# An mLSTM cell followed by a SwiGLU block: when k and q are first turned by 32 by 32 tiles, where weight words are joined, and the order of the first group

## The chip, the cores and the metric

The kernel runs on one core of a Trainium2 chip. The metric is the device time of one execution in microseconds (us); the time shown for a kernel is the median of its runs. A profiled execution is a further one, recorded by the hardware profiler; its span goes from the first to the last instruction. The engines are called as in the profile: PE multiplies matrices (PEld loads its stationary operand), DVE, ACT and POOL compute elementwise, and SP only issues transfers here. ACT also issues some transfers on its own queue.

## What is computed

```python
# q, k, v, o_gate: (4, 8, 768, 40) float32; i_gate, f_gate: (4, 8, 768) float32
for t in range(S):
    m_new = np.maximum(f_gate[:, :, t] + m, i_gate[:, :, t])
    f_stab, i_stab = np.exp(f_gate[:, :, t] + m - m_new), np.exp(i_gate[:, :, t] - m_new)
    m = m_new
    C = f_stab[:, :, None, None] * C + i_stab[:, :, None, None] * np.einsum('bhd,bhe->bhde', vt, kt)
    n = f_stab[:, :, None] * n + i_stab[:, :, None] * kt
    h_tilde = np.einsum('bhde,bhe->bhd', C, qt)
    denom = np.maximum(np.abs(np.einsum('bhd,bhd->bh', n, qt)[:, :, None]), 1.0)
    y[:, :, t] = h_tilde / (1.0 + np.exp(-o_gate[:, :, t])) / denom
x = y.transpose(0, 2, 1, 3).reshape(3072, 320)
g = x @ w_gate                      # (320, 1536), float64 in memory
out = (g / (1.0 + np.exp(-g)) * (x @ w_val)) @ w_out      # (3072, 320)
```

## The kernel before

The 768 time steps are cut into six groups of 128. For each group the cell is computed in its chunked form and gives 4 times 128 rows of x; `seam` turns them into xT; `hidden(g, m)` computes one twelfth of the hidden layer of a group (20 matrix instructions into two PSUM banks, then `AF.Silu` on ACT into `sg`, then a product on DVE); `project` or, in group 0, `project_all` multiplies with w_out, and `result` copies each of four blocks to `z_sb` on ACT and sends it out on SP. PE thus runs hidden(g, 0) to hidden(g, 11), then the projection of group g, and the cell of group g+1 is put between the hidden blocks of group g, in the lists `slots` and `after`, which say behind which block a step is written. Nothing reorders what is written: each engine's queue is run in the order of the program text, and `ahead` says which weight block is converted ahead of which hidden block.

PSUM has two rings of four banks. "gen" serves `hidden`, `project` and the first group's values; "cell" serves the scores, the state, the turns and the seams.

The weights come as 64-bit words and are made into float32 by integer steps. `piece_load(p)` brings a piece (the gate half on SP, the value half on ACT, both lines L161). `scale(j)` makes `top` and `low` from the two words of block j on ACT (L186, L188). `join(j)` makes `both` from `top` on DVE (L196, L197). `rounded(j)` adds `low` into the weight tile, on POOL or, for some blocks, on DVE (L204). The tiles `top`, `low` and `both` have one buffer each. Pieces 0 and 1 hold weight blocks 0 and 1, pieces 2 to 6 two blocks each, pieces 7 to 9 are w_out (blocks 12 to 17).

k and q are needed with the feature axis on the partitions. Group 0 does this with `first_turn` on PE, group 1 with `turn` (32 matrix instructions of PE and four copies for half of the heads), and groups 2 to 5 with `turn_squares`: the transfers of `load_squares` (16 for q and 16 for k, each a strip of 32 by 32 or 32 by 8 numbers) bring the data so that DVE's 32 by 32 transpose alone is enough. q's squares lie in `q_sb`, k's in `k_sq`.

The first group has its own functions (`first_mask` to `first_seam`), written between L540 and L582. `burn(n)` gives PE n idle products. `late_sums` and `late_maxima` prepare the gates of the five later groups, `late_turns` and `decay_rows`/`decay` what these need of it. `sig` is the sigmoid of the output gates on ACT.

Every transfer carries one of eight completion counters, in turn; a transfer that takes a counter waits for the transfer that had it before. The wait stands on the queue that issues it, so that on ACT the computing instructions written behind it wait too.

Of the kernel before, what the change touches and what calls it, by code (L numbers as in the profile page):

```python
# [11 lines left out]
I32 = mybir.dt.int32  # L12
# [12 lines left out]
def kernel(  # L25
# [102 lines left out]
    nc.sync.dma_start(out=i0, in_=spread_rows(i_gate))  # L128
    nc.scalar.dma_start(out=flat(f_sb), in_=gate_rows(f_gate)[:, L:])
    nc.scalar.dma_start(out=flat(i_sb), in_=gate_rows(i_gate)[:, L:])  # L130

# [3 lines left out]

    def piece_load(p, home=None):
        kind, m, n = PIECES[p]
        if kind == "gv":
            a, d = NKC, n * 128
            src = [(slice(i * HP, (i + 1) * HP), w[:, m * 128:(m + n) * 128].rearrange("(c p) f -> p c f", p=HP))  # L140
                   for i, w in enumerate((moe_w_gate, moe_w_val))]
            queues = (nc.sync, nc.scalar)
        else:
            a, d = n, DM
            src = [(slice(0, 128), moe_w_out[m * 128:(m + n) * 128].rearrange("(a p) d -> p a d", p=128))]
            queues = (nc.sync,)
# [34 lines left out]
    def scale(j):  # L181
        if j in blocks:
            lo, hi, dst = blocks[j]
            a, d = hi.shape[1], hi.shape[2]
            top = conv.tile([128, NKC * 128], F32, name="top", bufs=1).rearrange("p (a d) -> p a d", a=a)
            nc.scalar.mul(top, hi.bitcast(F32), 2.0 ** -112)  # L186
            low = conv.tile([128, NKC * 128], I32, name="low", bufs=1).rearrange("p (a d) -> p a d", a=a)
            nc.scalar.mul(low, lo, 2.0 ** -29)  # L188
            blocks[j] = (low, top.bitcast(U32), dst)

    def join(j):
        if j in blocks:
            lo, top, dst = blocks[j]
            a = dst.shape[1]
            both = conv.tile([128, NKC * 128], U32, name="both", bufs=1).rearrange("p (a d) -> p a d", a=a)
            nc.vector.tensor_scalar(both, top, scalar1=3, scalar2=None, op0=ALU.logical_shift_left)  # L196
            nc.vector.scalar_tensor_tensor(both, in0=top, scalar=0x80000000, in1=both, op0=ALU.bitwise_and,  # L197
                                           op1=ALU.bitwise_or)
            blocks[j] = (lo, both, dst)

    def rounded(j, eng=None):
        if j in blocks:
            lo, both, dst = blocks.pop(j)
            (eng or nc.gpsimd).tensor_tensor(dst.bitcast(I32), both.bitcast(I32), lo, op=ALU.add)  # L204

# [9 lines left out]
    load(o_sb, o_gate, 0, 0)  # L215
    load(o_sb, o_gate, 0, 1)

# [223 lines left out]

    def burn(n):
        t = bank("burn")
        for _ in range(n):
# [109 lines left out]
    first_turn(1, q_sb, qT, (A, V))  # L554
    piece_load(0)
    piece_load(1)
    first_own(1)
    first_values(1)
    first_x(1)
    first_scores(1)  # L560
    sig(0)
    sig(1)
    piece_load(2, h_sb[:, NH - NKC:])
    piece_load(3, wo_sb)
    burn(3)
    first_own(2)
    first_own(3)
    first_gate(0)
    first_x(2)
    first_x(3)  # L570
    first_gate(1)
    first_seam(0, (A, V, A))
    scale(0)
    piece_load(4)
    burn(5)
    join(0)
    first_seam(1, (A, A, A))
    rounded(0, V)
    first_state(0, A)
# [100 lines left out]
    def load_all(dst, a, n):  # L680
        for P in range(2):
# [9 lines left out]
    slots = {  # L691
        0: [run(first_state, 1, A), run(load_all, k_sb, k, 1), run(load_all, q_sb, q, 1), run(late_maxima)],
        1: [run(decay_rows), run(piece_load, 6, h_sb[:, NH - NKC:])],
        2: [run(late_turns), run(weights_load, 1)],
        3: [run(decay), run(load_all, v_sb, v, 1)],
        6: [run(turn, 0, (A, A), (A, V)), run(piece_load, 7)],
        7: [run(turn, 1, (A, A), (A, V)), run(weights_sub, 1, 0), run(weights_sub, 1, 1), run(weights_mask, 0),
            run(weights_mask, 1)],
        8: [run(weights_exp, 0), run(weights_exp, 1), run(weigh_values, G, 0), run(weigh_values, G, 1),
            run(piece_load, 8)],  # L700
        9: [run(do_scores), run(do_weigh, 0), run(load_all, o_sb, o_gate, 1)],
        10: [run(do_weigh, 1), run(do_add), run(do_state, 2, 0), run(do_state, 2, 1)],
        11: [run(do_attend, 1, 0), run(do_gather, 1, 0, False), run(piece_load, 9)],
    }
    for m in range(NFC):
        hidden(0, m, [run(convert, j, V if j in on_vector else None) for j in ahead[m]])
        for f in slots.get(m, ()):
            f()
    after = {
        0: [run(do_attend, 1, 1), run(convert, 14), run(sig, 0), run(sig, 1), run(do_gate, 0)],  # L710
        1: [run(do_gather, 1, 1), run(weights_load, 2), run(load_all, v_sb, v, 2),
            run(nc.gpsimd.memset, q_sb, 0.0)],
        2: [run(do_divide, 0), run(convert, 15)],
        3: [run(do_divide, 1), run(load_all, k_sb, k, 2), run(load_squares, q_sq, q, 2), run(load_all, o_sb, o_gate, 2)],
        4: [run(convert, 16), run(seam, 1, 0, (A, V, A, V))],
# [17 lines left out]
    nc.gpsimd.memset(k_sq, 0.0)  # L733
    load_squares(k_sq, k, 2)


    for g in range(1, NG):
        n, f = g + 1, g + 2
        slots = {m: [] for m in range(NFC)}
        if n < NG:  # L740
            slots[2 if g == 1 else 0] = [run(turn_squares, q_sq, qT)]
            slots[2 if g == 1 else 1] += [run(turn_squares, k_sq, kT)]
            slots[3] = [run(do_scores), run(do_weigh, 0)]
# [59 lines left out]
```

## Time and profile before

| what | us |
|---|---|
| median of 3 runs | 574.75 (573.42 to 575.8) |
| profiled execution, whole | 574.24 |
| its span, first to last instruction | 572.5 |
| PE busy with matrix instructions | 562.0 |
| DVE / ACT / POOL busy | 221.9 / 142.9 / 105.8 |
| bytes moved by DMA | 40.46 MB |
| granted TensorE clock, mean | 0.991 |

The span and the time of the profiled execution differ by 1.74 us, which lie outside the instructions. A line of the timeline reads: start, duration, engine, line of the kernel, operation, result and operands with their shapes, count, and in brackets the idle time before it and what ended it. "x40" behind a matrix instruction of L619 stands for two hidden blocks. Instructions of PE are pipelined, so a busy PE may still wait inside a merged line.

### The profile page before, as it was taken

What the parts mean: (1) busy time and instruction counts of PE and PEld (TensorE: products, weight loads), DVE (VectorE), ACT (ScalarE), POOL (GpSimd) and SP (SyncE); (2) the same over time, 40 slices, a digit from 0 to 9 for tenths busy, and PEclk for the clock granted to TensorE, in tenths of its full rate; (3) what the DMA queues carried; (4) which work ended last, traced back from release to release, by engine and by line L of the source; (5) the groups of instructions that cost most, each with busy time, mean ns of one, the idle gap of its engine ahead of it and who ended that gap; (6) DMA issues with size and microseconds to landing.
All of it is one profiled execution on the core that took longest, in us unless ns stands there. A gap on an engine that the chain in (4) does not pass through costs nothing.

```text
span 572.5 us, 11789 instructions
## 1 busy us (share of the span) xinstructions
PE 562.0 (98%) x5151; PEld 326.4 (57%) x5151; DVE 221.9 (39%) x378; ACT 142.9 (25%) x221; POOL 105.8 (18%) x103
## 2 busy tenths in 40 slices
PE   9999998999899999999999999999999999999997
PEld 4955454764555576455567445567455567544475
DVE  5776595870434620434630433640332630011100
ACT  3366554435201115110114201014211010111100
POOL 2132345464101132002132001232001110000000
PEclk9999998999899999999999999999999999999999
DMA  8999992495457620354440263360000000000000
GB/s 124 179 285 179 174 264 93 86 119 104 55 67 88 112 45 24 53 53 72 81 75 24 35 70 49 64 115 24 12 2 1 2 2 26 21 2 0 1 22 24
DMA packets 180987, 40.46 MB, mean 71 GB/s; under 512 B 171496, under 2 KB 176104, under 8 KB 180936
## 3 DMA queue, kind: packets, MB, share of 16 engines
q1 hardware_dynamic: 178356, 35.55, 37.8%
q10 hardware_dynamic: 2580, 4.16, 3.4%
q8 instruction: 40, 0.66, 0.5%
q14 instruction: 11, 0.09, 0.1%
HBM read 35.68 MB, written 4.01 MB: 69 GB/s over the span
## 4 chain that ended last, share of the span: by engine, by line
PE 86%; DMA 5%; SPq 4%; ACT 3%; issue 1%; DVE 1%; POOL 0%; ACTq 0%; DVEq 0%; POOLq 0%
PE gv_ps L619 50%; PE o_ps L635 23%; PE o_ps L642 4%; SPq L113 3%; DMA raw<-in_moe_w_val_dram 3%; DMA h_sb<-in_moe_w_gate_dram 2%; PE inter L369 2%; PE intra L374 2%; PE add L350 2%; PE sp L329 1%; PE tp_x L415 1%; DMA out_dram<-z_sb 1%; DVE w_sb L336 0%; ACT L624 0%; ACT L436 0%
## 5 line engine op out<-in xcount | busy, mean ns | idle before, releaser
L619 PE MATMUL gv_ps<-xT,wgv_sb 64*128 64x512 f32 x1440 | 323.3, 599 | 3.9 <-ACT sg L624 2.8
L619 PEld LDWEIGHTS gv_ps<-xT,wgv_sb 64*128 64x128 f32 x1440 | 142.6, 188 | 161.2 <-issue 151.5
L625 DVE TENSOR_TENSOR h_sb<-sg,gv_ps 128x512 f32<-128x512 f32 x72 | 49.4, 687 | 290.3 <-ACT sg L624 269.3
L635 PE MATMUL o_ps<-wo_sb,h_sb 128*128 128x320 f32 x480 | 130.5, 433 | 0.0
L635 PEld LDWEIGHTS o_ps<-wo_sb,h_sb 128*128 128x128 f32 x480 | 90.8, 190 | 38.2 <-issue 0.8
L624 ACT ACTIVATE sg<-gv_ps 128x512 f32<-128x512 f32 x72 | 42.9, 597 | 264.7 <-PE gv_ps L619 264.7
L359 POOL TENSOR_TENSOR C<-C,dec 128x328 f32<-128x328 f32 x20 | 14.5, 735 | 156.4 <-DVE C L361 156.4
L629 ACT COPY z_sb<-o_ps 128x320 f32<-128x320 f32 x24 | 10.2, 426 | 116.2 <-PE o_ps L635 102.7
L432 POOL TENSOR_SCALAR_AFFINE_SELECT w_sb<-w_sb 64x1024 f32<-64x1024 f32 x20 | 28.1, 1406 | 27.0 <-DVE w_sb L427 26.0
L642 PE MATMUL o_ps<-wo_sb,h_sb 128*128 128x320 f32 x96 | 26.9, 437 | 0.0
L395 POOL TENSOR_TENSOR o_sb<-o_sb,y_sb 128x640 f32<-128x640 f32 x10 | 14.2, 1428 | 48.5 <-DVE y_sb L386 48.5
L642 PEld LDWEIGHTS o_ps<-wo_sb,h_sb 128*128 128x128 f32 x96 | 17.9, 190 | 7.2
L386 DVE TENSOR_TENSOR y_sb<-y_sb,intra 64x328 f32<-64x328 f32 x40 | 19.7, 492 | 1.0
L339 POOL TENSOR_TENSOR vw_sb<-v_sb,w_sb 128x656 f32<-128x656 f32 x10 | 12.8, 1302 | 34.2 <-issue 25.8
L204 POOL TENSOR_TENSOR wgv_sb<-both,low 128x640 int32<-128x640 int32 x8 | 13.4, 1671 | 24.7 <-DVE both L197 24.7
L197 DVE SCALAR_TENSOR_TENSOR both<-top,both 128x640 uint32<-128x640 uint32 x18 | 15.7, 870 | 0.6
L369 PEld LDWEIGHTS inter<-C,qT 64*64 64x64 f32 x640 | 10.2, 134 | 7.3 <-issue 6.8
L389 DVE TENSOR_SCALAR den<-den 128x16 f32<-128x16 f32 x10 | 14.0, 1402 | 0.3
L196 DVE TENSOR_SCALAR both<-top 128x640 uint32<-128x640 uint32 x18 | 10.5, 581 | 8.6 <-ACT top L186 6.7
L350 PEld LDWEIGHTS add<-vw_sb,k_sb 64*64 64x64 f32 x640 | 10.4, 135 | 5.7 <-issue 4.9
L361 DVE TENSOR_TENSOR C<-C,add 128x328 f32<-128x328 f32 x20 | 9.9, 493 | 9.3 <-POOL C L359 9.3
L204 POOL TENSOR_TENSOR wo_sb<-both,low 128x640 int32<-128x640 int32 x6 | 10.2, 1700 | 15.7 <-DVE both L197 12.2
(124 smaller groups left out, 367.0 us busy)
## 6 DMA issues: line engine op xcount, KB each, us to landing
w_sb<-M_dram SPq DMA_DIRECT2D x10, 512.0 KB, 6.2
k_sb<-in_k_dram SPq DMA_DIRECT2D x12, 320.0 KB, 6.4
v_sb<-in_v_dram SPq DMA_DIRECT2D x12, 320.0 KB, 4.9
o_sb<-in_o_gate_dram SPq DMA_DIRECT2D x12, 320.0 KB, 6.7
raw<-in_moe_w_out_dram SPq DMA_DIRECT2D x3, 1280.0 KB, 7.2
out_dram<-z_sb SPq DMA_DIRECT2D x24, 160.0 KB, 1.8
q_sb<-in_q_dram SPq DMA_DIRECT2D x32, 64.0 KB, 2.5
k_sq<-in_k_dram SPq DMA_DIRECT2D x32, 64.0 KB, 2.5
```

The lines of the kernel that those rows point to most:

```text
L113: nc.sync.dma_start(out=dst[:, heads(P), 0:D], in_=tokens(a, c, P))
L197: nc.vector.scalar_tensor_tensor(both, in0=top, scalar=0x80000000, in1=both, op0=ALU.bitwise_and, op1=ALU.bitwise_or)
L204: (eng or nc.gpsimd).tensor_tensor(dst.bitcast(I32), both.bitcast(I32), lo, op=ALU.add)
L350: nc.tensor.matmul(ps[i][half(two), a, :], lhsT=k_sb[half(i), h, :], rhs=vw_sb[half(i), h, :], start=True, stop=True)
L369: nc.tensor.matmul(inter[two][half(i), a, :], lhsT=qT[half(two), P * UA + a, half(i)], rhs=state(2 * n + i)[half(two), P * UA + a, :], sta ...
L386: nc.vector.tensor_tensor(t, t, intra[i][half(c)], op=ALU.add)
L432: nc.gpsimd.affine_select(w, w, compare_op=ALU.is_ge, fill=NEG, base=0, pattern=[[0, UH], [1, SUB]], channel_multiplier=-1)
L619: nc.tensor.matmul(ps[i], lhsT=wgv_sb[half(i), m, PAIRS[kc][i], :], rhs=x[half(i), kc, :], start=(kc == 0), stop=(kc == NKC - 1))
L624: nc.scalar.activation(sg, ps[0], AF.Silu)
L625: nc.vector.tensor_tensor(hid(g, m), sg, ps[1], op=ALU.mult)
L635: nc.tensor.matmul(p, lhsT=hid(g, m)[:, ts(u, L)], rhs=wo_sb[:, m, :], start=(m == 0), stop=(m == NFC - 1))
L642: nc.tensor.matmul(ps[u], lhsT=hid(g, m)[:, ts(u, L)], rhs=wo_sb[:, m, :], start=(m == 0), stop=(m == NFC - 1))
```

## The change

Five things are changed.

1. Group 2 is turned by `turn` on PE in the first two slots of group 1; squares are loaded and used from group 3 on. The loads of q's and k's squares for group 2 (32 transfers) become two plain loads of q (those of k were there already, for the state). The clearing of `q_sb` moves from group 0's projection to behind the second turn.
2. `join` writes into the weight tile itself, and `rounded` adds to it in place; `both` is gone and `low` has two buffers. Block 0 is rounded on POOL and no longer on DVE.
3. The second half of the output gates is loaded behind weight piece 0; the gates of the later groups (`f_sb`, `i_sb`) are loaded from ACT behind `sig(0)` and no longer at the start. The value halves of pieces 2 and 3 are issued on SP and no longer on ACT.
4. In the first group `scale(0)` stands ahead of `sig(1)`, `join(0)` and `rounded(0)` among the last values; `burn(8)` on a "gen" bank replaces `burn(5)` on a "cell" bank; one copy of the second seam goes from ACT to DVE.
5. In the slots of group 0 `late_maxima`, `late_turns`, `decay_rows` and `decay` stand one block later, both turns one block earlier, and the second `do_weigh` one block earlier, behind the first.

```diff
-    nc.scalar.dma_start(out=flat(f_sb), in_=gate_rows(f_gate)[:, L:])
-    nc.scalar.dma_start(out=flat(i_sb), in_=gate_rows(i_gate)[:, L:])
...
-    def piece_load(p, home=None):
+    def piece_load(p, home=None, second=nc.scalar):
...
-            queues = (nc.sync, nc.scalar)
+            queues = (nc.sync, second)
...
-            low = conv.tile([128, NKC * 128], I32, name="low", bufs=1).rearrange("p (a d) -> p a d", a=a)
+            low = conv.tile([128, NKC * 128], I32, name="low").rearrange("p (a d) -> p a d", a=a)
...
-            both = conv.tile([128, NKC * 128], U32, name="both", bufs=1).rearrange("p (a d) -> p a d", a=a)
+            both = dst.bitcast(U32)
...
-            lo, both, dst = blocks.pop(j)
-            (eng or nc.gpsimd).tensor_tensor(dst.bitcast(I32), both.bitcast(I32), lo, op=ALU.add)
+            lo, dst = blocks.pop(j)
+            (eng or nc.gpsimd).tensor_tensor(dst, dst, lo, op=ALU.add)
...
-    load(o_sb, o_gate, 0, 1)
...
     piece_load(0)
+    load(o_sb, o_gate, 0, 1)
     piece_load(1)
     first_own(1)
     first_values(1)
     first_x(1)
     first_scores(1)
     sig(0)
+    nc.scalar.dma_start(out=flat(f_sb), in_=gate_rows(f_gate)[:, L:])
+    nc.scalar.dma_start(out=flat(i_sb), in_=gate_rows(i_gate)[:, L:])
+    piece_load(2, h_sb[:, NH - NKC:], nc.sync)
+    piece_load(3, wo_sb, nc.sync)
+    scale(0)
     sig(1)
-    piece_load(2, h_sb[:, NH - NKC:])
-    piece_load(3, wo_sb)
     burn(3)
     first_own(2)
     first_own(3)
     first_gate(0)
     first_x(2)
+    join(0)
     first_x(3)
+    rounded(0)
     first_gate(1)
     first_seam(0, (A, V, A))
-    scale(0)
+    burn(8, "gen")
     piece_load(4)
-    burn(5)
-    join(0)
-    first_seam(1, (A, A, A))
-    rounded(0, V)
+    first_seam(1, (V, A, A))
     first_state(0, A)
     convert(1)
     piece_load(5)
...
-        0: [run(first_state, 1, A), run(load_all, k_sb, k, 1), run(load_all, q_sb, q, 1), run(late_maxima)],
-        1: [run(decay_rows), run(piece_load, 6, h_sb[:, NH - NKC:])],
-        2: [run(late_turns), run(weights_load, 1)],
-        3: [run(decay), run(load_all, v_sb, v, 1)],
-        6: [run(turn, 0, (A, A), (A, V)), run(piece_load, 7)],
-        7: [run(turn, 1, (A, A), (A, V)), run(weights_sub, 1, 0), run(weights_sub, 1, 1), run(weights_mask, 0),
-            run(weights_mask, 1)],
+        0: [run(first_state, 1, A), run(load_all, k_sb, k, 1), run(load_all, q_sb, q, 1)],
+        1: [run(late_maxima), run(piece_load, 6, h_sb[:, NH - NKC:])],
+        2: [run(weights_load, 1), run(load_all, v_sb, v, 1), run(decay_rows)],
+        3: [run(late_turns)],
+        4: [run(decay)],
+        5: [run(turn, 0, (A, A), (A, V))],
+        6: [run(turn, 1, (A, A), (A, V)), run(piece_load, 7)],
+        7: [run(weights_sub, 1, 0), run(weights_sub, 1, 1), run(weights_mask, 0), run(weights_mask, 1)],
...
-        9: [run(do_scores), run(do_weigh, 0), run(load_all, o_sb, o_gate, 1)],
-        10: [run(do_weigh, 1), run(do_add), run(do_state, 2, 0), run(do_state, 2, 1)],
+        9: [run(do_scores), run(do_weigh, 0), run(do_weigh, 1), run(load_all, o_sb, o_gate, 1)],
+        10: [run(do_add), run(do_state, 2, 0), run(do_state, 2, 1)],
...
-        1: [run(do_gather, 1, 1), run(weights_load, 2), run(load_all, v_sb, v, 2),
-            run(nc.gpsimd.memset, q_sb, 0.0)],
+        1: [run(do_gather, 1, 1), run(weights_load, 2), run(load_all, v_sb, v, 2)],
...
-        3: [run(do_divide, 1), run(load_all, k_sb, k, 2), run(load_squares, q_sq, q, 2), run(load_all, o_sb, o_gate, 2)],
+        3: [run(do_divide, 1), run(load_all, k_sb, k, 2), run(load_all, q_sb, q, 2), run(load_all, o_sb, o_gate, 2)],
...
-    load_squares(k_sq, k, 2)
...
-            slots[2 if g == 1 else 0] = [run(turn_squares, q_sq, qT)]
-            slots[2 if g == 1 else 1] += [run(turn_squares, k_sq, kT)]
+            slots[0] = [run(turn, 0, (A, V), (A, V))] if n == 2 else [run(turn_squares, q_sq, qT)]
+            slots[1] = [run(turn, 1, (A, V), (A, V))] if n == 2 else [run(turn_squares, k_sq, kT)]
+            if n == 2:
+                slots[1].append(run(nc.gpsimd.memset, q_sb, 0.0))
```

## The prediction, written before the changed kernel had run

> **What bounds the kernel now.** I read the shares of the chain first, then the chain in order of time, then PE's timeline wherever PE was idle or slow, and last what the engine named there had been doing.
>
> ```profile
> PE 86%; DMA 5%; SPq 4%; ACT 3%; issue 1%; DVE 1%; POOL 0%; ACTq 0%; DVEq 0%; POOLq 0%
> ```
>
> PE is the chain, and the rest lies at the beginning: in order of time there is nothing but PE from 145 us to the last copy. There a pair of hidden blocks takes 8.78 us (4.39 each) and a projection 26.0, group after group. So the change can gain or lose only at the start of PE's hidden work, at the idle places before 157 us, and by PE work added or taken. These are the places:
>
> ```profile
> 33.45 4.56 PE L619 MATMUL gv_ps<-xT,wgv_sb 64*128 64x512 f32 x20
> 49.59 4.74 PE L619 MATMUL gv_ps<-xT,wgv_sb 64*128 64x512 f32 x20 [0.99 <-POOL wgv_sb L204]
> ...
> 84.94 5.71 PE L619 MATMUL gv_ps<-xT,wgv_sb 64*128 64x512 f32 x20
> 90.58 1.34 PE L350 MATMUL add<-vw_sb,k_sb 64*64 64x41 f32 x64
> 93.33 0.28 PE L350 MATMUL add<-vw_sb,k_sb 64*64 64x41 f32 x2 [1.41 <-DVE w_sb L336]
> 93.94 1.14 PE L350 MATMUL add<-vw_sb,k_sb 64*64 64x41 f32 x62 [0.32 <-DVE w_sb L336]
> 95.00 6.26 PE L619 MATMUL gv_ps<-xT,wgv_sb 64*128 64x512 f32 x20
> ...
> 133.52 8.85 PE L619 MATMUL gv_ps<-xT,wgv_sb 64*128 64x512 f32 x40
> 145.17 11.27 PE L619 MATMUL gv_ps<-xT,wgv_sb 64*128 64x512 f32 x40 [2.80 <-ACT sg L624]
> ```
>
> Measured against 4.39 us a block, hidden(0,10) at 84.94 loses 1.25 (to the start of add at 90.58); add takes 4.49 instead of the 2.0 of later groups and loses 2.5; hidden(0,11) at 95.0 loses 1.8; PE idles 2.80 before 145.17, and the pair after it loses 2.5. With the 0.99 before 49.59 that is 11.8 us. The reader is to see that a slow block follows two of the idle spells, 1.7 us in add and 2.80, and none follows the 0.99 or the 1.25.
>
> Why PE idles at 142.4 is on ACT and SP:
>
> ```profile
> 118.66 11.73 SPq L313 DMA_DIRECT2D q_sb<-in_q_dram  x16
> 130.48 1.83 SPq L113 DMA_DIRECT2D o_sb<-in_o_gate_dram  x2
> 132.46 5.22 SPq L630 DMA_DIRECT2D out_dram<-z_sb  x4
> ```
> ```profile
> 132.01 0.96 ACT L629 COPY z_sb<-o_ps 128x320 f32<-128x320 f32 x2 [9.66 <-PE o_ps L642]
> 136.42 0.80 ACT L629 COPY z_sb<-o_ps 128x320 f32<-128x320 f32 x2 [3.45 <-DMA out_dram<-z_sb]
> 144.52 1.08 ACT L624 ACTIVATE sg<-gv_ps 128x512 f32<-128x512 f32 x2
> ```
>
> Sixteen square loads hold SP for 11.7 us, the output gates are issued behind them, and the first output block (3.86 us to landing in the chain, median 1.8 of all) shares the DMA with these. z has two buffers, so the third copy waits; three table loads, exp and sigmoid stand behind it on ACT, and only then the first Silu, 8.1 us after the third copy began.
>
> **What the Trainium skill says.** "TensorE: Matmul & The Clock Gate", Part 1, says PE's clock falls to half after an idle window of about 3.4 us and needs a busy one to recover, the window running freely. The trace agrees in kind: behind both long spells weight loads take 0.35 or 0.61 us a pair instead of 0.19; it shows 1.7 us of idle among small products as enough. The same Part says ACT and DVE run their queues strictly in order; here ACT stood from 49.00 to 50.17 before issuing piece 6, until piece 5 landed at 50.10. "DMA: Bandwidth & Descriptors", Specifications, wants 512 B for line rate; the squares are strips of 128 and 32 B, the k, q, v and o rows 160 B, and 10:20, full of the latter, moved 153 GB/s where 30:40, full of weights, moved 321. "SBUF — State Buffer", Who interferes with whom, says a DVE instruction with two SBUF inputs contends with POOL; L197 took 0.83 us, and 1.63 beside POOL's masks.
>
> **The change part by part.**
>
> *The start.* Before, hidden(0,0) starts at 33.45, when the seam copies end (33.19). Now ACT's queue decides. The built program's list of waits puts in front of `scale(0)` the load of i_sb, which waits for piece 1's gate half, and in front of the second seam's copies the issue of piece 4's value half, which waits for piece 2's value half. I date both by bytes. o0 landed at 21.2 (issue 14.21, 7.0 to landing); without f_sb, i_sb (0.16 MB, about 0.7 us) and the two value halves that shared from 18.9 (about 1.1 us) it lands near 19.4. Behind it up to piece 1 come 1.31 MB of weights and o1's 0.33 MB: at about 185 GB/s, between 153 and 198 (20:30), 8.8 us, so near 28.2. Piece 2's 1.31 MB at 321 GB/s takes 4.1 more, near 32.5. So scale(0) (1.57) runs from 28.3, sig(1) ends near 30.7; join(0) (1.35) puts x(3), gate(1) (2.0) and the POOL copy at 32.8; the second seam's transposes (1.3) and `first_state` (1.06) bring PE to 35.2, its copies being done at 35.0. burn(8), at 0.4 each as in burn(5)'s 2.02, ends at 31.6 and is hidden under this wait. The start slips by 1.75 us. Bounds: 33.2 if everything landed early enough, 37.5 if the landings slip by 2.3.
>
> *To hidden(0,4).* Before, it starts at 54.88 with the decay product (0.55) done. Now 35.2 + 4 x 4.39 + 1.06 (`first_state`) + 0.8 (`late_turns`) = 54.6, and the decay product is still to come: 55.2. The 0.99 stall goes, since late_maxima (2.8 us of DVE, then exp) no longer stands ahead of block 3. It now stands ahead of block 4: Silu ends near 45.8, the maxima near 49.4, exp 50.1, piece 6's issue 50.7 (it waits for piece 5, which I put at 48 to 50), scale, join and POOL 54.4. That is level with PE, so any slip shows. Net loss 0.3.
>
> *Joining in place.* It removes waits of ACT for POOL (0.8 to 0.95 each) in work beside PE, and 4.39 us of PE a block covers it: nothing, except at blocks 10 and 11, where DVE holds Silu of hidden(0,8). There `low` frees ACT, but weights_sub and POOL's masks still stretch DVE, and I leave the 1.25 us loss as it is. Without that cover it would gain up to 1.25.
>
> *do_weigh one block earlier.* The four products (0.64 each) run at 89.3 to 91.9 ahead of join(12), so add finds its banks and takes 2.0; hidden(0,11) runs 93.1 to 97.5 at full clock instead of ending at 101.2. What is late next: join(12) and Silu's product now stand behind the four products, POOL's block 12 ends near 94.9, and the state chain of POOL and DVE (4.6 us, as from 93.64 to 98.27) ends at 99.4. The second half of attend's banks waits for it, about 1.0 us. attend ends at 100.4, before at 103.2: gain 2.8.
>
> *Group 2's turns.* The 32 square loads leave SP; two q loads (about 2 us each by the k loads' 3.73 for two) replace 11.7 us before the outputs. The first output lands in 1.8 us, the third copy starts at 134.3 on the old scale, Silu of hidden(1,0) ends at 143.0. PE has one turn (1.0) more and reaches the second turn at 143.3. Its banks are freed by ACT's copies behind that Silu and DVE's behind its product: k's at 144.4, q's at 145.1. So hidden(1,2) starts at 145.6, 0.4 later than before, with 2.0 us of turns done, and the pair runs warm, the longest wait being 1.1 us: it ends at 154.4 against 156.45. Gain 2.05. DVE's squares at 152.85 lay beside PE, so taking them gains nothing. The q_sb clearing (1.8 us on POOL) comes at 146, long before the states at 167 and the squares' use past 225.
>
> **Sum.** +0.3 - 2.8 - 2.05 = -4.55 us. On the profiled execution: span 568.0, and with the 1.74 outside it 569.7. The median shown stands 0.5 above the profiled execution, so I forecast 570.2.
>
> **Rivals.**
> Given back to the clock (0.22). The start has 1.3 us of idle and small products ahead of hidden(0,0), attend 1.0, the second turn 1.3: each shorter than the 1.7 that was enough before, but the window runs freely. Each slow window costs 1.8 to 2.5. Two of them: 570.2 + 4 = 574.2, no change. For it: both slow blocks of the trace; against: the 0.99 and 1.25 that had none.
> Slower (0.18). ACT's queue at the start: transfers that wait for landings now stand in front of the seam copies, where before none did. If pieces 1 and 2 land some 6 us later than I reckon (value halves starved by SP's ring, or the 160 B rows at 153 GB/s deciding), hidden(0,0) starts near 41.5 on a cold clock: +6.3 + 1.8 - 4.55 = 3.55, so 578.3. It decides once the start passes 42.6, or 40.8 with the cold window.
> More than the sum (0.12). DVE gets through blocks 10 and 11 in time (1.25) and the turn's banks come free early (up to 1.3), the start slips less (1): 566.7.
> The forecast itself has 0.48, with its own range 568 to 572.5.
>
> **How the numbers follow.** A measurement of this kernel cannot tell less than about 0.5%, 2.9 us, from no change: the borders are 571.9 and 577.6. Faster gets nearly all of the forecast and all of the last rival, 0.58; no change the clock's rival and the edges, 0.26; slower 0.16. The range goes from 566.5, the last rival, to 576, past the clock's rival and halfway to the slower one.
>
> **What would show it.** PE's timeline: first hidden block near 35 us; no idle of over 1.5 us near 92 or 143; add near 2.0 us; hidden(0,11) near 4.4; a wait of about 1 us in attend and before hidden(1,2). SP: no square loads before group 1. It is wrong if ACT stands in front of L159 past 35 us, if hidden(1,2) begins with slow weight loads, or if PE after 160 us takes other times per block than before.

## The result, and the profile after

The changed kernel took 575.36 us (median of 20 runs, 572.71 to 576.99), the kernel before, run beside it, 574.91 (572.54 to 579.33). The ratio is 1.0 with a 95% interval of 0.9981 to 1.0019: no change that this measurement can tell. The profiled execution of the changed kernel took 576.29, with a span of 574.5; that of before 574.24 and 572.5. The traces can therefore be compared stage by stage, and the 2.0 us between the two spans have to come out. Only two of the changed kernel's 20 runs took longer than its profiled execution, so most of these 2.0 us are spread: the medians differ by 0.45.

The shares of the chain that ended last, after:

```profile
PE 87%; DMA 6%; DVE 3%; ACT 2%; POOL 1%; issue 1%; SPq 0%; ACTq 0%; DVEq 0%; POOLq 0%
```

PE still carries it. SP's issuing has left the chain (4% before), since the sixteen square loads of group 2 are gone. DMA and DVE have grown, and what they hold of the chain lies ahead of 150 us. PE's timeline after shows the places (start, duration, line, operation, count, and idle time before with its releaser):

```profile
31.99 2.31 PE L533 MATMUL tp_x<-ident,x_sb 128*128 128x128 f32 x10 [2.60 <-DVE x_sb L516]
34.23 1.94 PE L524 MATMUL add<-vw_sb,k_sb 128*64 128x41 f32 x32
36.10 4.91 PE L618 MATMUL gv_ps<-xT,wgv_sb 64*128 64x512 f32 x20
40.94 1.13 PE L524 MATMUL add<-vw_sb,k_sb 128*64 128x41 f32 x32
43.57 13.15 PE L618 MATMUL gv_ps<-xT,wgv_sb 64*128 64x512 f32 x60 [1.50 <-POOL wgv_sb L201]
...
59.32 6.50 PE L618 MATMUL gv_ps<-xT,wgv_sb 64*128 64x512 f32 x20 [1.88 <-POOL wgv_sb L201]
66.22 4.56 PE L618 MATMUL gv_ps<-xT,wgv_sb 64*128 64x512 f32 x20
...
98.08 2.08 PE L346 MATMUL add<-vw_sb,k_sb 64*64 64x41 f32 x128
100.09 4.56 PE L618 MATMUL gv_ps<-xT,wgv_sb 64*128 64x512 f32 x20
...
149.92 8.86 PE L618 MATMUL gv_ps<-xT,wgv_sb 64*128 64x512 f32 x40
158.71 2.10 PE L325 MATMUL sp<-qT,kT 64*64 64x64 f32 x128
```

Two readings. The places that the prediction wanted mended are mended: `add` takes 2.08 in one piece, hidden(0,11) and the pair that begins with hidden(1,2) run at full clock. New losses stand ahead of them: hidden(0,0) starts 2.65 us later than before, PE waits 1.50 ahead of hidden(0,1) and 1.88 ahead of hidden(0,4), and hidden(0,4) then takes 6.50 instead of 4.56. Stage by stage, from the starts of the same work in both timelines:

| stage | before | after | difference |
|---|---|---|---|
| to the start of hidden(0,0) | 33.45 | 36.10 | +2.65 |
| from there to the start of hidden(0,5) | 25.82 | 30.12 | +4.30 |
| hidden(0,5) to group 0's scores | 23.65 | 23.75 | +0.10 |
| group 0's scores to its projection (`do_weigh`, `add`, `attend`) | 20.28 | 17.20 | -3.08 |
| projection of group 0 | 30.32 | 30.56 | +0.24 |
| hidden(1,0) to group 1's scores (group 2's turns) | 22.97 | 20.98 | -1.99 |
| the rest of the span | 416.01 | 415.79 | -0.22 |

So 5.1 us were won where they had been expected, and 6.95 were lost in the first 66 us.

The late start of hidden(0,0) is PE's own. Before, the second seam's transposes and `first_state` ran like this:

```profile
31.15 1.31 PE L537 MATMUL tp_x<-ident,x_sb 128*128 128x128 f32 x10
32.39 1.13 PE L528 MATMUL add<-vw_sb,k_sb 128*64 128x41 f32 x32
```

After, the same products begin 0.84 later and take 4.11 us instead of 2.30, because PE had only half of its clock. The trace records the granted clock. After, it is half from 32.73 to 36.14, across these products, and from 60.04 to 63.45, in hidden(0,4); before, from 27.22 to 30.63, from 95.48 to 98.89 (hidden(0,11)) and from 146.68 to 150.09 (hidden(1,2)); everywhere else up to the end of the program it is full. Each stretch is 3.41 us long. The two after (span, busy time of PE, PEld, DVE, ACT and POOL with counts, PE clock, DMA busy share, GB/s):

```profile
32.73:36.14 3.41, 3.41 (x42) 2.98 (x40) 0.90 (x2) 0.00 (x0) 0.00 (x0) 0.50 1.06 212
60.04:63.45 3.41, 3.41 (x10) 2.67 (x9) 3.38 (x7) 2.06 (x4) 1.55 (x1) 0.50 1.56 139
```

What follows does not hang on this start, since PE then waits 1.50 us for block 1 all the same. What it waits for there and at 59.32 is on ACT, whose timeline after has these lines:

```profile
27.74 0.78 ACT L184 ACTIVATE top<-raw 128x640 f32<-128x640 f32 x1 [2.75 <-DMA raw<-in_moe_w_gate_dram]
...
36.86 0.62 ACTq L159 DMA_DIRECT2D raw<-in_moe_w_val_dram  x1
37.52 0.86 ACT L117 COPY xT<-tp_x 128x512 f32<-128x512 f32 x2 [6.93 <-DMA h_sb<-in_moe_w_val_dram]
...
40.82 0.61 ACTq L159 DMA_DIRECT2D raw<-in_moe_w_val_dram  x1
...
54.77 0.60 ACTq L159 DMA_DIRECT2D h_sb<-in_moe_w_val_dram  x1
55.42 0.79 ACT L184 ACTIVATE top<-wo_sb 128x640 f32<-128x640 f32 x1 [2.09 <-DMA raw<-in_moe_w_gate_dram]
```

ACT stands idle for 6.93 us because the value half of piece 4 cannot be issued before the value half of piece 2 has landed (36.8), and the seam's copies and the conversion of block 1 are written behind that issue. Piece 1's value half, which block 1 needs, was no earlier: it landed at 37.1.

At 54.77 the same happens with piece 6: its issue waits for piece 5, and the conversion of block 4 is written behind it. The bracket at 55.42, and the profile's chain with it, name the gate half of piece 5. The landings say that it was the value half (first the value half, issued at 40.82, then the gate half, issued at 43.95; the last number is us from issue to landing):

```profile
raw<-in_moe_w_val_dram ACTq DMA_DIRECT2D x1, 640.0 KB, 13.9
```
```profile
raw<-in_moe_w_gate_dram SPq DMA_DIRECT2D x1, 640.0 KB, 12.6
```

The value half landed at 54.69, 0.08 before piece 6 was issued, and both carry the same counter. The gate half landed at 56.6, when block 4 was already being converted. The value half came late because ACT had issued it late: at 40.82, against 35.42 before, once piece 3's gate half had landed (40.7), one of the four halves that SP's queue now carries one behind the other. It landed 4.6 us later than before (50.10).

The stretch from 30 to 40 us, first before, then after:

```profile
30.00:40.00 10.00, 9.94 (x104) 5.70 (x104) 7.35 (x10) 6.15 (x11) 3.15 (x2) 0.97 1.05 321
```
```profile
30.00:40.00 10.00, 7.87 (x60) 4.97 (x62) 4.07 (x9) 3.07 (x7) 1.82 (x2) 0.83 1.08 207
```

The DMA engines are as busy as before (1.08 against 1.05) and move a third less.

### The profile page after: what moved, and what is told of

It reads as the page before. It is cut to its first block, busy times and chain, and to the rows that moved or that the text cites. A ratio compares the mean times of both kernels' runs of the same rounds, so it can differ in the third digit from the quotient of the medians.

```text
span 574.5 us, 11872 instructions
## 1 busy us (share of the span) xinstructions
PE 561.7 (98%) x5216; PEld 326.3 (57%) x5218; DVE 219.7 (38%) x378; ACT 143.7 (25%) x224; POOL 107.6 (19%) x104
## 3 DMA queue, kind: packets, MB, share of 16 engines
q1 hardware_dynamic: 166260, 36.20, 39.5%
## 4 chain that ended last, share of the span: by engine, by line
PE 87%; DMA 6%; DVE 3%; ACT 2%; POOL 1%; issue 1%; SPq 0%; ACTq 0%; DVEq 0%; POOLq 0%
PE gv_ps L618 48%; PE o_ps L634 23%; PE o_ps L641 4%; DMA wo_sb<-in_moe_w_val_dram 4%; DMA raw<-in_moe_w_gate_dram 2%; PE intra L370 2%; PE inter L365 2%; PE sp L325 1%; PE add L346 1%; PE tp_x L411 1%; PE burn L441 1%; PE first_y L502 1%; DVE wgv_sb L194 1%; PE tp_kq L481 1%; DVE wgv_sb L193 1%
## 5 line engine op out<-in xcount | busy, mean ns | idle before, releaser
L618 PEld LDWEIGHTS gv_ps<-xT,wgv_sb 64*128 64x128 f32 x1440 | 140.5, 188 | 160.0 <-issue 152.0
L428 POOL TENSOR_SCALAR_AFFINE_SELECT w_sb<-w_sb 64x1024 f32<-64x1024 f32 x20 | 28.2, 1408 | 26.1 <-DVE w_sb L423 25.1
L201 POOL TENSOR_TENSOR wgv_sb<-wgv_sb,low 128x640 int32<-128x640 int32 x9 | 14.9, 1654 | 33.8 <-DVE wgv_sb L194 30.0
L193 DVE TENSOR_SCALAR wgv_sb<-top 128x640 uint32<-128x640 uint32 x12 | 9.0, 746 | 13.0 <-ACT top L184 13.0
L184 ACT ACTIVATE top<-raw 128x640 f32<-128x640 f32 x12 | 9.6, 799 | 14.1 <-issue 5.3
L423 DVE TENSOR_TENSOR w_sb<-g_T,w_sb 128x1024 f32<-128x1024 f32 x10 | 13.1, 1350 | 0.0
L201 POOL TENSOR_TENSOR wo_sb<-wo_sb,low 128x640 int32<-128x640 int32 x6 | 10.2, 1707 | 15.0 <-DVE wo_sb L194 10.5
L332 DVE TENSOR_TENSOR w_sb<-sp,w_sb 128x512 f32<-128x512 f32 x20 | 12.7, 681 | 0.0
```

Of the source, the lines that this page charges most:

```text
L201: (eng or nc.gpsimd).tensor_tensor(dst, dst, lo, op=ALU.add)
L428: nc.gpsimd.affine_select(w, w, compare_op=ALU.is_ge, fill=NEG, base=0, pattern=[[0, UH], [1, SUB]], channel_multiplier=-1)
L618: nc.tensor.matmul(ps[i], lhsT=wgv_sb[half(i), m, PAIRS[kc][i], :], rhs=x[half(i), kc, :], start=(kc == 0), stop=(kc == NKC - 1))
```

## The experiments

The theory after this reading: the losses lie in the start and are made by transfers. A gate half goes to partitions 0 to 63, a value half to partitions 64 to 127; put one behind the other on SP, they come later, and ACT, which issues transfers between its copies, stands in front of computing work until they land. The rivals: the new order of the first group costs by itself, whatever the loads; the new slots of group 0, with `late_maxima` one block later, cost by themselves; ACT's queue does not matter and the number of issuing queues does.

**The value halves back on ACT, all else as changed.**

```diff
-    piece_load(2, h_sb[:, NH - NKC:], nc.sync)
-    piece_load(3, wo_sb, nc.sync)
+    piece_load(2, h_sb[:, NH - NKC:])
+    piece_load(3, wo_sb)
```

> The changed kernel with the value halves of pieces 2 and 3 issued on ACT again, all else as changed. Theory (gate and value halves of a piece move side by side only when they are on two queues; on SP alone they come one behind the other): DMA moves over 300 GB/s at 32 to 41 us instead of 207, piece 3's value half lands near 40 instead of 43.9, piece 5 near 50 instead of 55.4, hidden(0,4) starts near 55.5 instead of 59.3, the whole about 572. The second seam still waits for piece 4's issue, so hidden(0,0) stays near 36. Rival (the order of the loads at the start, with i_sb ahead of scale(0), sets the loss): DMA stays near 200 GB/s, hidden(0,4) stays at 59, the whole at 575.

Measured: 574.96 us, ratio to the kernel before 0.9994 (0.9981 to 1.0008). The expectation fell: hidden(0,0) started later still, at 39.24, and took 7.00 us, the clock being half from 33.95 to 44.19. ACT's timeline shows what the expectation had left out:

```profile
29.94 0.60 ACTq L159 DMA_DIRECT2D wo_sb<-in_moe_w_val_dram  x1
30.59 0.80 ACT L184 ACTIVATE top<-raw 128x640 f32<-128x640 f32 x1 [8.39 <-DMA raw<-in_moe_w_gate_dram]
```

In the new order the issues of both value halves stand ahead of `scale(0)`, and the second of them waits for piece 1's gate half. `scale(0)` starts at 30.59, after at 27.74. Moving the halves to SP had bought that much; the issue and the order cannot be judged one without the other.

**The whole start as before, everything else as changed.** The loads of the gates, the second output gates, pieces 2 and 3 and the steps of the first group are written as in the kernel before; turns, joining in place and slots stay changed.

```diff
     nc.sync.dma_start(out=i0, in_=spread_rows(i_gate))
+    nc.scalar.dma_start(out=flat(f_sb), in_=gate_rows(f_gate)[:, L:])
+    nc.scalar.dma_start(out=flat(i_sb), in_=gate_rows(i_gate)[:, L:])
...
     load(o_sb, o_gate, 0, 0)
+    load(o_sb, o_gate, 0, 1)
...
-    piece_load(2, h_sb[:, NH - NKC:], nc.sync)
-    piece_load(3, wo_sb, nc.sync)
-    scale(0)
     sig(1)
+    piece_load(2, h_sb[:, NH - NKC:])
+    piece_load(3, wo_sb)
...
-    burn(8, "gen")
+    scale(0)
     piece_load(4)
-    first_seam(1, (V, A, A))
+    burn(5)
+    join(0)
+    first_seam(1, (A, A, A))
+    rounded(0, V)
```

> The changed kernel with the whole start as before (order of the first group, loads of f_sb, i_sb and the second output gates, value halves on ACT), keeping the turns of group 2, the joins in place and the new slots. Theory (the start lost what the later parts gained): hidden(0,0) at 33.5, hidden(0,4) near 55, the pair before the first scores of group 1 ends 4 us or more earlier than before, the whole 570 to 572. Rival (the later parts gain nothing outside the one profiled execution): the whole 575, as before.

Measured: 572.7 us, 0.9944 (0.9925 to 0.9963), faster than both, though not quite by the 570 to 572 expected. hidden(0,0) started at 33.09. But PE waited 3.35 us ahead of hidden(0,4), and that block took 7.59, most of it at half clock (55.27 to 62.10). This profiled execution was the slowest but one of 18 (574.61). On ACT:

```profile
51.59 0.60 ACTq L161 DMA_DIRECT2D h_sb<-in_moe_w_val_dram  x1
52.30 0.79 ACT L186 ACTIVATE top<-wo_sb 128x640 f32<-128x640 f32 x1 [2.57 <-DMA raw<-in_moe_w_gate_dram]
```

So the second stand, piece 6's issue ahead of block 4's conversion, does not need the late landings: it is there with the old loads as well, because in the new slots block 4, and no longer block 3, follows `late_maxima` and this issue at once.

**Piece 4 issued behind the second seam, all else as changed.**

```diff
     burn(8, "gen")
-    piece_load(4)
     first_seam(1, (V, A, A))
+    piece_load(4)
     first_state(0, A)
```

> The changed kernel with piece 4 issued behind the second seam instead of ahead of it, so that ACT no longer stands in front of the seam copies. Theory (the landing of piece 5, not the seam, sets hidden(0,4)): hidden(0,0) starts near 34.3 instead of 36.1, piece 5 still lands near 55, hidden(0,4) still starts near 59, the whole 575. Rival (ACT's wait at the seam is the loss): all blocks move up with it, the whole 573.

Measured: 575.67 us, 0.9999 (0.9975 to 1.0023). hidden(0,0) started at 34.60, 1.5 earlier:

```profile
31.98 1.63 PE L533 MATMUL tp_x<-ident,x_sb 128*128 128x128 f32 x10
33.54 1.13 PE L524 MATMUL add<-vw_sb,k_sb 128*64 128x41 f32 x32
```

The transposes began when they had begun after (31.99), but at full clock; the half-clock stretch lay at 27.58 to 30.99. So these 1.5 us are the clock's; whether the edit moved the stretch, or chance did, one trace does not tell. The issue of piece 4 waited until 36.84 as before and still stood ahead of block 1's conversion: PE waited 2.55 ahead of hidden(0,1), which started at 42.77 (43.57 after). hidden(0,4) started at 58.43 (59.32 after), again at half clock: 6.29.

**Both of these edits together**, the value halves on ACT and piece 4 behind the second seam.

```diff
-    piece_load(2, h_sb[:, NH - NKC:], nc.sync)
-    piece_load(3, wo_sb, nc.sync)
+    piece_load(2, h_sb[:, NH - NKC:])
+    piece_load(3, wo_sb)
...
-    piece_load(4)
     first_seam(1, (V, A, A))
+    piece_load(4)
```

> The changed kernel with both: value halves of pieces 2 and 3 on ACT, and piece 4 issued behind the second seam. Theory: hidden(0,0) near 34.3, hidden(0,4) near 54.5, the whole about 570.5. Rival (order of loads): 574 to 575.

Measured: 574.47 us, 0.998 (0.9964 to 0.9995), and the expectation missed: hidden(0,0) at 38.73. `scale(0)` waited until 30.10, as with the value halves on ACT alone. The clock was half from 34.16 to 40.99. From hidden(0,1) on nothing waited, and hidden(0,4) started at 59.20 at full clock, so the late start alone was left.

**Only group 2's turns on PE, in the kernel before.** Its lines are those of the change:

```diff
-        3: [run(do_divide, 1), run(load_all, k_sb, k, 2), run(load_squares, q_sq, q, 2), run(load_all, o_sb, o_gate, 2)],
+        3: [run(do_divide, 1), run(load_all, k_sb, k, 2), run(load_all, q_sb, q, 2), run(load_all, o_sb, o_gate, 2)],
...
-    load_squares(k_sq, k, 2)
...
-            slots[2 if g == 1 else 0] = [run(turn_squares, q_sq, qT)]
+            slots[0] = [run(turn, 0, (A, V), (A, V))] if n == 2 else [run(turn_squares, q_sq, qT)]
```

> The kernel before with the turns of group 2 alone (no square loads for group 2, plain loads of q). Theory (the prediction's step for group 1 holds): the idle of 2.80 us and the slow pair behind it go, 2 us of turns come, the pair before the first scores of group 1 ends about 2.0 us earlier, the whole 572.9. Rival (the wait of the third output copy stays, because it does not come from the squares): 575 or above.

Measured: 573.3 us, 0.9962 (0.9936 to 0.9987). From hidden(1,0) to group 1's scores its trace has 134.10 to 155.10, 21.0 us against 22.97: the same 2 us as in the changed kernel.

**Only the new slots of group 0, in the kernel before.** The lines that matter for the result:

```diff
-        0: [run(first_state, 1, A), run(load_all, k_sb, k, 1), run(load_all, q_sb, q, 1), run(late_maxima)],
-        1: [run(decay_rows), run(piece_load, 6, h_sb[:, NH - NKC:])],
+        0: [run(first_state, 1, A), run(load_all, k_sb, k, 1), run(load_all, q_sb, q, 1)],
+        1: [run(late_maxima), run(piece_load, 6, h_sb[:, NH - NKC:])],
...
-        9: [run(do_scores), run(do_weigh, 0), run(load_all, o_sb, o_gate, 1)],
-        10: [run(do_weigh, 1), run(do_add), run(do_state, 2, 0), run(do_state, 2, 1)],
+        9: [run(do_scores), run(do_weigh, 0), run(do_weigh, 1), run(load_all, o_sb, o_gate, 1)],
+        10: [run(do_add), run(do_state, 2, 0), run(do_state, 2, 1)],
```

> The kernel before with the new slots of group 0 alone. Theory (the slots gain about 2.2 us from the first add on, and lose more at hidden(0,4), because late_maxima and piece 6's issue now stand ahead of block 4 on ACT): hidden(0,4) starts near 56 and runs slow, the add of group 0 takes 2.0 us, the whole 576 to 577. Rival (the loss at hidden(0,4) in the changed kernel comes from the late landing of piece 5 alone): hidden(0,4) near 55, the whole 573.

Measured: 576.34 us, 1.0016 (0.9992 to 1.0039). `add` took 2.55 instead of 4.49, so the `do_weigh` part worked here too. PE waited 2.48 ahead of hidden(0,4), which took 6.46, although piece 5's value half landed at 49.9, as early as before (50.1). The slots win and lose about the same.

**Piece 6 issued one slot later, behind block 4's conversion; once with the start as before, once in the changed kernel.**

```diff
-        1: [run(late_maxima), run(piece_load, 6, h_sb[:, NH - NKC:])],
-        2: [run(weights_load, 1), run(load_all, v_sb, v, 1), run(decay_rows)],
+        1: [run(late_maxima)],
+        2: [run(piece_load, 6, h_sb[:, NH - NKC:]), run(weights_load, 1), run(load_all, v_sb, v, 1), run(decay_rows)],
```

> The kernel with the start undone (as in e2_start_undone), and piece 6 issued one block later, behind hidden(0,2), so that ACT converts block 4 before it waits for piece 5. Theory: hidden(0,4) starts near 54 instead of 56.2 and at full clock, the whole 568.5 to 569.5. Rival (block 4 waits for late_maxima, not for piece 6's issue): hidden(0,4) near 55.5, the whole 571 to 572.5.

> The changed kernel with piece 6 issued one block later, behind hidden(0,2). Theory: ACT converts block 4 from 53.4 instead of 55.4, hidden(0,4) starts near 57.5 without a wait and at full clock, the whole 571.5. Rival (the landings set the pace, and the wait only moves to the next block): a wait and a slow block at hidden(0,5) or (0,6), the whole 575.

Measured: 569.16 us, 0.9893 (0.9865 to 0.9921), with the start as before; 573.07 us, 0.9962 (0.9946 to 0.9977), in the changed kernel. ACT with the start as before:

```profile
49.11 0.74 ACT L282 ACTIVATE keep<-keep 32x640 f32<-32x640 f32 x1 [3.02 <-DVE keep L281]
49.76 0.76 ACT L186 ACTIVATE top<-wo_sb 128x640 f32<-128x640 f32 x1
50.53 0.60 ACTq L161 DMA_DIRECT2D h_sb<-in_moe_w_val_dram  x1
```

The conversion now follows the exponential at once. hidden(0,4) waited 0.67 and took 4.81; in the changed kernel it started at 57.77, as expected, without a wait, and took 4.56, though the whole came 1.6 above the 571.5 expected. One line moved is worth 0.5% with the start as before (0.9944 to 0.9893) and 0.4% in the changed kernel, where the late start (hidden(0,0) at 36.20) stays. The second stand is shown.

**The loads alone, in the kernel before: both value halves on SP; and piece 2 whole on SP, piece 3 whole on ACT.**

```diff
-    piece_load(2, h_sb[:, NH - NKC:])
-    piece_load(3, wo_sb)
+    piece_load(2, h_sb[:, NH - NKC:], nc.sync, nc.sync)
+    piece_load(3, wo_sb, nc.sync, nc.sync)
```
```diff
+    piece_load(2, h_sb[:, NH - NKC:], nc.sync, nc.sync)
+    piece_load(3, wo_sb, nc.scalar, nc.scalar)
```

> The kernel before with the value halves of pieces 2 and 3 on SP, nothing else. Theory (one behind the other on one queue, each into 64 partitions): DMA near 205 GB/s from 30 to 40 us instead of 321, hidden(0,4) starts 1 to 2.5 us later, the whole 576 to 578. Rival (the low rate in the changed kernel comes from the order of its loads): over 300 GB/s, the whole 575.

> The kernel before with both halves of piece 2 on SP and both halves of piece 3 on ACT, so that two queues run side by side but always into the same 64 partitions (gate with gate, value with value). Theory A (two queues are what makes gate and value halves fast): DMA still moves 300 GB/s or more from 31 to 41 us. Theory B (the two halves of the partitions are what makes them fast): 200 to 215 GB/s, as in the changed kernel. The whole 574 to 577 either way.

Measured: 578.63 us, 1.0054 (1.0038 to 1.0069), with the value halves on SP, slower by about 3 us from that edit alone, and above the 576 to 578 expected. From 30 to 40 us it moved 211 GB/s. Piece 1's value half shared its 64 partitions with piece 2's and landed at 36.8; ACT waited 4.66 for it, and PE 3.42 ahead of hidden(0,1), which then ran at half clock (42.25 to 45.66):

```profile
41.81 10.55 PE L619 MATMUL gv_ps<-xT,wgv_sb 64*128 64x512 f32 x40 [3.42 <-POOL wgv_sb L204]
```

With a whole piece on each queue: 575.53 us, 1.0 (0.9977 to 1.0023), and 295 GB/s over the ten microseconds. By its number this speaks for two queues, but the mean mixes two things. In three shorter stretches of the same trace:

```profile
33.00:35.00 2.00, 2.00 (x12) 0.97 (x11) 1.97 (x3) 0.39 (x1) 0.76 (x1) 1.00 1.04 365
35.00:37.00 2.00, 2.00 (x30) 1.03 (x28) 1.97 (x2) 0.00 (x0) 2.00 (x2) 1.00 1.07 253
37.00:39.50 2.50, 2.50 (x28) 1.44 (x26) 0.69 (x4) 0.86 (x2) 0.39 (x1) 1.00 1.05 356
```

The trace records each packet with its queue and size, and counting the bytes of each queue tells which half is moving. In the first stretch piece 2's value half runs beside piece 3's gate half, in the last piece 4's gate half beside piece 3's value half: different partitions. For about one microsecond between them both queues carry gate halves, piece 4's on SP and piece 3's on ACT: both are moving, together at 195 to 225 GB/s. Packets of 2 KB took about 155 ns there, 92 in the fast stretches. The kernel with the value halves on SP has a longer example: from 38 to 42 us piece 3's value half on SP and piece 4's on ACT moved side by side, 98 GB/s each. The changed kernel has another, 4.4 us in which piece 2's value half on SP and piece 1's on ACT moved 196 GB/s together.

In all of this the gate halves also come from another tensor than the value halves. What excludes the tensor, and the number of queues, is w_out: its pieces come from one tensor, go to all 128 partitions and are issued on SP alone. First the two value halves side by side, then w_out in the kernel before:

```profile
38.00:42.00 4.00, 0.58 (x16) 0.46 (x14) 3.93 (x4) 1.35 (x3) 2.81 (x2) 1.00 1.07 200
```
```profile
76.00:81.00 5.00, 5.00 (x26) 2.26 (x24) 4.83 (x5) 1.14 (x3) 4.35 (x3) 1.00 1.03 400
```

So two queues on one half of the partitions are no faster than one; the gate half and the value half side by side are, and one queue that fills both halves is faster still.

**The changed order of the first group with the loads of before**, and piece 6 one slot later as above. Against the kernel of 569.16 us the first group's order alone differs:

```diff
-    sig(1)
     piece_load(2, h_sb[:, NH - NKC:])
     piece_load(3, wo_sb)
+    scale(0)
+    sig(1)
...
     first_x(2)
+    join(0)
     first_x(3)
+    rounded(0)
...
-    scale(0)
+    burn(8, "gen")
     piece_load(4)
-    burn(5)
-    join(0)
-    first_seam(1, (A, A, A))
-    rounded(0, V)
+    first_seam(1, (V, A, A))
```

> The fastest so far (start undone, piece 6 later) with the changed order of the first group (first block scaled ahead of the second sigmoid, joined and rounded among the last values, longer burn, one seam copy on DVE), and the loads as before. Theory (the order alone costs, since block 0's words land near 28 us and the second sigmoid, the gates and the seam now stand behind them): hidden(0,0) starts near 35 instead of 33.2, the whole 571. Rival (only the moved loads cost): hidden(0,0) at 33.5 or earlier, the whole 569.

Measured: 573.44 us, 0.9954 (0.9929 to 0.9979), against 569.16 with the old order. In its profiled execution (span 567.6, against 567.4 with the old order) hidden(0,0) starts at 34.99 instead of 33.24, and the gap is down to 0.47 by hidden(0,5), because nothing waits ahead of hidden(0,4). From 30 to 40 us it moved 347 GB/s. The order alone thus delays the start by 1.75 us, and almost nothing of it is left later. The medians differ by 4.3, and that goes with the granted clock: the ten of its 22 runs with a mean clock of 0.996 or 0.997 took 569.28 to 571.04, the twelve with 0.994 or less took 573.00 to 576.08. All six runs with the old order had 0.996 or more and took 568.22 to 571.44. Whether the new order brings the half clock about more often is not shown: six runs are few.

**Group 2's second turn one slot later**, in the kernel with the start as before and piece 6 later.

```diff
-            slots[1] = [run(turn, 1, (A, V), (A, V))] if n == 2 else [run(turn_squares, k_sq, kT)]
+            slots[2 if n == 2 else 1] = [run(turn, 1, (A, V), (A, V))] if n == 2 else [run(turn_squares, k_sq, kT)]
```

The clearing of `q_sb` moves along with it.

> The fastest so far (start undone, piece 6 later) with group 2's second turn one block later, behind hidden(1,2), so that PE does not wait for the copies of the first turn. Theory: the wait of about 1.1 us ahead of the second turn goes and the whole is 568. Rival (hidden(1,2) then waits for its banks, because Silu is as late as before): the same 569.2.

Measured: 567.25 us (566.93 to 571.24), 0.9855 (0.9823 to 0.9886). This is the quickest kernel of the study, faster than before and after; it has six runs. In the changed kernel the second turn is cut into pieces that wait for the copies of the first turn, 0.2 to 0.36 at a time (here in PE's timeline after):

```profile
147.99 0.27 PE L290 MATMUL tp_kq<-ident,k_sb 64*128 64x64 f32 x1 [0.36 <-ACT kT L117]
149.43 0.71 PE L290 MATMUL tp_kq<-ident,q_sb 64*128 64x64 f32 x15 [0.24 <-DVE qT L119]
```

One block later no such wait is left: hidden(1,0) to the scores took 20.34 us (129.30 to 149.64), in the changed kernel 20.98 and in the one of 569.16 us 20.99. So 0.65 us are the edit's. The spans of these last two differ by 1.6; 1.04 of that lies ahead of hidden(0,5), where both kernels are the same, and cannot be put down to the edit.

## Why the prediction was wrong

It forecast 570.2 us; the median came out 5.2 above, inside its range and outside the likeliest case. By its own steps:

*do_weigh one block earlier* was priced at -2.8 and brought -3.08 in the stage from the scores to the projection. `add` gave 2.41 of it and hidden(0,11) 1.70, by running at full clock; hidden(0,10) and `attend` took 0.45 and 0.58 back. What was foretold to be late next, about 1.0 ahead of `attend`, was 0.29. The mechanism in `add` is right, and the slots alone show it too (2.55). The 1.70 is in part luck: "a slow block follows" the idle of 1.7 us in `add` in the kernel before, but with group 2's turns alone the same idle (1.41 and 0.32) stood there, and hidden(0,11) ran at full clock:

```profile
97.42 4.56 PE L619 MATMUL gv_ps<-xT,wgv_sb 64*128 64x512 f32 x20
```

*Group 2's turns* were priced at -2.05 and brought -1.99 in the changed kernel and 2.0 in the stage when alone. hidden(1,2) ran at full clock, as said. This step is right in mechanism and size. Both steps survive in the kernel that undoes the start and moves piece 6: 569.16.

The miss lies ahead of hidden(0,5). The sum had +0.3 us for all of it, and +6.95 came; these 6.65 are the whole difference between the forecast span of 568.0 and the measured 574.5, but for 0.1. Two steps made it.

*The start* failed at one term: "Piece 2's 1.31 MB at 321 GB/s takes 4.1 more, near 32.5", and with it at the date of piece 1, "near 28.2". That date held for piece 1's gate half, on which `scale(0)` hung (27.74, forecast 28.3). Piece 1's value half landed at 37.1 and piece 2's at 36.8. 321 GB/s had been read in a stretch in which the gate half of one piece and the value half of another moved side by side, and the change takes just that away. With the 199 GB/s that a single half moves, 1.31 MB take 6.6, and piece 1's value half (0.33 MB), which went to the same partitions at the same time, 1.6 more: 36.4. "SBUF — State Buffer", section "Door 1: The DMA port swizzle", of the Trainium skill has the reason: it gives 196 GB/s for partitions 0 to 63 and 328 for all 128, since partitions 0 to 63 reach half of the ports. The trace agrees with the first number (199) and lies above the second (400 for w_out). The same page's section "Can I just issue two DMAs to hit both halves?" says that two transfers at once, to partition 0 and partition 64, gain 6%. Here they gain 77% (352 GB/s over the 6.5 us in which both queues of the kernel before moved 2 KB packets, against 199 for one half), and the measurement decides.

What the term cost shows at hidden(0,1). By the prediction's numbers it starts at 40.65 (35.2 + 4.39 + 1.06); it started at 43.57, 2.92 later, because ACT stood until 36.86 and block 1 was converted behind it. The forecast for hidden(0,0), 35.2, missed by only 0.90, and by another way: it had `burn(8)` end at 31.6, at 0.4 us each, which is what the products of `burn(5)` took in the half-clock stretch of the kernel before. At full clock PE was through at 29.39, stood for 2.60, and then had half clock. With the new order and the old loads the start slipped by 1.75 us, as forecast.

*To hidden(0,4)*: "It now stands ahead of block 4", said of `late_maxima`, with piece 6's issue waiting "for piece 5, which I put at 48 to 50", and "That is level with PE, so any slip shows. Net loss 0.3." The wait was seen and its size was not. Piece 5's value half landed at 54.69, because its issue on ACT hung on SP's queue of four halves; that date never entered the sum. PE waited 1.88, and hidden(0,4) ran at half clock and lost another 1.94 (6.50 against 4.56). With the 2.92 this is 6.74, which covers the miss. The slots alone show that even good landings would have lost here: 2.48 of waiting and 6.46 for the block. To call the step level with PE and then cost it at nothing was the error; a wait plus a block at half clock, some 4 us, belonged in the sum.

*Joining in place* was costed at nothing. No run had it alone, so that stays untested; the kernels that keep it and undo the start reach the forecast without it showing.

*The rivals.* "Given back to the clock" forecast 574.2, close to what came, and two half-clock stretches, as many as came. One lay at the start, as it said, but PE waited behind it anyway; the other took its 1.94 in hidden(0,4), which it had not named; attend and the second turn kept full clock. So its number is in part luck. "Slower, via ACT's queue" named the right mechanism, transfers that wait for landings ahead of the seam copies. Its place and price were off: hidden(0,0) came at 36.1 and not 41.5, and the loss showed at hidden(0,1). The mark set beforehand, that the forecast is wrong if ACT stands in front of L159 past 35 us, was reached (36.86). What came is this second rival with 2.92 us at hidden(0,1), plus the second stand of ACT and its block at half clock, against gains that were right.

## What to carry to other kernels

When a transfer is moved to another queue, price it by what moves beside it: the rate read in the old schedule belongs to the old pairing of destinations, and two halves of the partitions should be kept in flight together. A duration read in a half-clock stretch, like `burn`'s 0.4 us, belongs to that stretch. A transfer issue on an engine that also computes is a place where that engine can stand, so put it behind the computing work that is due next, and date the landing that it will wait for, from the counter that it takes and not from the name in the bracket. A step that comes out "level" with the busy engine is to be costed with its wait and with the slow clock after it, not at nothing.

## What had not been expected of the hardware

The halves of the partitions, and not the queues, set the rate: 199 GB/s with one half moving, 352 with the two halves on two queues, 400 with one queue filling both, and 195 to 225 with two queues on the same half, at a DMA busy share of 1.03 to 1.08 throughout. The busy share does not show the difference; the GB/s beside it does.

A transfer that is issued is not a transfer that moves. In the kernel before, ACT issued piece 2's value half at 23.94, and by the packet records it began to move near 31 us; from 24 to 30 us mostly one queue moved at a time (195 to 207 GB/s), although both had work. In the changed kernel ACT issued piece 4's value half at 36.86, and its queue moved nothing from 37.7 to 43.4, while SP's moved 209 GB/s. Nothing in the records says what held the other.

hidden(0,4), or hidden(0,3) in its place, took 6.13 to 7.59 us instead of 4.56 after waits of 1.76 to 3.35 us in six kernels; after 0.67 and 0.99 it took 4.81 and 4.74. In each of the six the clock record has half clock in that block, for 3.41 us (6.83 where it took 7.59), and in the other two it has none there. The wait alone does not decide: with piece 4 issued later, hidden(0,1) ran at full clock after 2.55. "TensorE: Matmul & The Clock Gate", Part 1, puts the idle window at about 3.4 us; behind the small products ahead of hidden(0,4) here, about 1.8 were enough.
